# A transformer block on one core: attention spreads on two queues, halved score sums for the last chunk, and x loaded ahead of the weights

## The chip, the cores and the metric

The kernel runs on one core of a Trainium2 chip. The metric is the device time of one execution in microseconds (us). The names of the engines in the profile are PE (TensorE, matmuls), DVE (VectorE), ACT (ScalarE), POOL (GpSimd) and SP (SyncE, which here only issues DMA). DMAs are issued from the queues of SP, ACT and POOL.

## The reference

The block has 2048 positions of 512 features in bf16: a layer norm, a sliding dilated attention with 32 heads of 16 features, a residual, a second layer norm, a gated ReLU feed-forward layer with 1376 hidden features, and a residual.

```python
W, dil = 8, 2
idx = pos[:, None] - (jnp.arange(W) * dil)[None, :]      # 8 keys: s, s-2, ..., s-14
logits = einsum("bhsd,bhswd->bhsw", q, k[idx]) * Dh**-0.5  # masked where idx < 0
o = einsum("bhsw,bhswd->bhsd", softmax(logits), v[idx])
h = x + o @ wo
n = layernorm(h)
out = h + (relu(n @ W_gate) * (n @ W_up)) @ W_down
```

## The kernel before, in words

The positions are cut into four chunks of 512 (`tk` = 0 to 3). Features lie on partitions, positions along the free dimension. A chunk goes through these steps; the line numbers are those of the profile:

- layer norm 1: statistics on DVE (L466, L469), ln and exp on ACT (L479, L483), normalised rows on DVE (L501, chunks 0 and 2) or ACT (L498, chunks 1 and 3). The rows are transposed on PE (L530) and copied by ACT (L546) or, once, by DVE (L544). Chunk 3's four row blocks are instead transposed by DMAs on SP's queue (L519).
- q, k, v: matmuls (L571), copied out of PSUM by ACT (L579).
- q*k products on DVE. Chunks 1 to 3 use tiles of 128x4096 (L619), two feature groups by four window places by 512; chunk 0 uses halves of those (L634). A half `hf` of the window (four of the eight keys) takes two such tiles. They are summed over a head's features by matmuls with a 0/1 matrix `sel` (L625), 16 for each half; the exponential is on ACT (L683). In chunk 0 a small mask follows on DVE (L686).
- spreads: the exponentials (32 heads on 32 partitions per window place) are copied to 128 partitions by DMAs, `big<-ex` (L743), four for each half, 128 KB each. The table `BCD` names the queue of each: S is SP, A is ACT, P is POOL.
- a*v products on DVE (L775; halves in chunk 0, L790), summed over the window by a tree of adds (L778). In chunks 0 to 2 the first add, 128x2048, is a DMA with accumulation on POOL's queue (L818). The last step writes a tile of `quad` (L782 in chunk 0, L812 in the others).
- output projection on PE (L854), residual (L863, L865), layer norm 2, gate and up matmuls (L927, L894), their copies and product (L931, L934, L955), down matmuls (L977) and the second residual.

`setup()` issues the loads ahead of all that. SP and ACT each load a block of x, then a quarter of the q and k weights `wqk_sb`, twice. Three one-row copies on POOL (L333, L336, L338) read a piece of what has been loaded and write into a tile that is loaded next; so chunk 1's x, the v weights and the x of chunks 2 and 3 are not issued before the earlier loads have landed. `NFILL` matmuls on a dummy tile stand between the first transposes on PE.

The order of the work on each engine is written down: every step gets a number from the table `RANK`, and a list planner with durations for each kind of step puts the steps of each engine in order by it. Its durations are constants in the code. Every engine works strictly in its order, so a step that waits holds up all that stands behind it on its engine or queue.

Of the kernel before, what the change touches and what calls it, by code (L numbers as in the profile page):

```python
# [8 lines left out]
P = 128  # L9
# [193 lines left out]
def kernel(  # L203
# [22 lines left out]
    BCD = {(0,0):"SSSS",(0,1):"SSSS",(1,0):"SSSS",(1,1):"SSSS",(2,0):"SSSS",(2,1):"SSSS",(3,0):"SSSS",(3,1):"SSSS"}  # L226
    PRE = ()
    PRD = ()
    ODA = (0, 1)
# [82 lines left out]
    def setup():  # L312

        w3_r = A_wqkv.rearrange("(dt p) f -> p dt f", p=P)
        for i in range(2):
            for n, q in enumerate((nc.sync, nc.scalar)):
                j = 2 * i + n
                q.dma_start(x_sm[:, j:j + 1, :], x_rows[:, j:j + 1, :])
                q.dma_start(wqk_sb[:, j:j + 1, :], w3_r[:, j:j + 1, 0:2 * D])  # L319
# [13 lines left out]
        nc.gpsimd.tensor_copy(out=x_sm[0:1, BPC:2 * BPC, 0:1], in_=x_sm[0:1, 3, 0:BPC])  # L333
        for j in range(BPC, 2 * BPC):
            nc.sync.dma_start(x_sm[:, j:j + 1, :], x_rows[:, j:j + 1, :])
        nc.gpsimd.tensor_copy(out=wv_sb[0:1, 0, 0:1], in_=wqk_sb[0:1, 3, 0:1])  # L336
        nc.sync.dma_start(wv_sb[:], w3_r[:, :, 2 * D:3 * D])
        nc.gpsimd.tensor_copy(out=x_sm[0:1, 2 * BPC, 0:1], in_=x_sm[0:1, 2 * BPC - 1, 0:1])  # L338
# [34 lines left out]
    TDD, TDL = 1.25, 1.5  # L373
    NWARM, NFILL = 56, (13, 10, 0)
    NHALF = 6
    XT = (3.55, 3.4, 6.1, 5.85, 9.0, 9.3, 9.6, 10.0, 15.2, 16.75)
    WT = (7.7, 7.7, 5.6, 12.05, 18.0, 24.95, 21.45, 28.8)
# [4 lines left out]
    BDI = {"S": 0.63, "A": 0.65, "P": 0.95}  # L382
# [16 lines left out]
    MM, TP = 0.2165, 0.057  # L399
    SW = 0.21  # L400
    PEL = 0.22
    A5, A10, AX, AS = 0.485, 0.91, 0.75, 0.21
# [151 lines left out]
    for tk in range(NCK):  # L554
# [50 lines left out]
        for hf in range(2):  # L605
            sc, ex = Buf(at_s), Buf(ex_s)
            scd, prd = [], []
            for t in range(0, NT, 2):
# [13 lines left out]
                def f_sc(t=t, sc=sc, pb=pb):  # L622
                    for u in range(2):
                        for g in range(4):
                            nc.tensor.matmul(sc.t[g * HB:(g + 1) * HB, :], lhsT=sel[:],  # L625
                                             rhs=pb.t[:, 4 * u + g, :], start=(t + u == 0),
                                             stop=(t + u == NT - 1), tile_position=(0, g * HB))

                if tk in PRS:
                    def f_p1(u, t=t, hf=hf, pb=pb, qT=qT, s0=s0):  # L630
                        kb = kT[:, t + u, PADL + s0 - 4 * hf * DIL: PADL + s0 - 4 * hf * DIL + CS]
                        k4 = bass.AP(tensor=kb.tensor, offset=kb.offset,
                                     ap=[list(kb.ap[0]), [-DIL, 4]] + [list(y) for y in kb.ap[1:]])
                        V.tensor_tensor(out=pb.t[:, 4 * u:4 * u + 4, :],  # L634
                                        in0=qT.t[:, t + u, :].unsqueeze(1).to_broadcast([P, 4, CS]), in1=k4, op=ALU.mult)

                    for u in range(2):
                        a = add(("pr%d%s" % (hf, "ac"[u]), tk), "DVE", D20, lambda u=u, f=f_p1: f(u),
                                [d[t + u] for d in (qd, kd, kp)], apr, take=[pb], use=[qT], lat=DL)
                        prd.append((a, pb, f_sc if u else lambda: None))  # L640
                else:
                    a = add(("pr%d" % hf, tk), "DVE", D40, f_pr, [d[k] for k in (t, t + 1) for d in (qd, kd, kp)],
                            apr, take=[pb], use=[qT], lat=DL)
                    prd.append((a, pb, f_sc))
# [29 lines left out]
            elif tk in MERGE:  # L674
                scd = [add(("sc%d" % hf, tk), "PE", 4 * MM + SW, lambda p=prd: [f() for _, _, f in p],
                           [a for a, _, _ in prd], apr, take=[sc], use=[b for _, b, _ in prd], lat=PEL)]
            else:
                for a, pb, f in prd:
                    scd.append(add(("sc%d" % hf, tk), "PE", 2 * MM + SW, f, [a] + scd[-1:], apr,
                                   take=[sc], use=[pb], lat=PEL))  # L680
# [52 lines left out]
        for w0 in range(0, W, BCN):  # L733
            hf = w0 // 4
            if (tk, hf) in BCD:
                for eng, q in (("SP", nc.sync), ("ACT", nc.scalar), ("POOL", nc.gpsimd)):
# [4 lines left out]
                    def f_bd(ws=ws, q=q, w0=w0, ab=ab, ex=exs[hf]):  # L741
                        for w in ws:
# [3 lines left out]
                                   take=[ab], use=[exs[hf]], lat=0.77,  # L746
# [102 lines left out]
        for j in range(BPC):  # L849
# [20 lines left out]
            if tk in RPE:  # L870
                a = add(("rs%d" % j, tk), "ACT", 0.57, f_rs, [a], base + 50, take=[sm], use=[od], lat=AL)
            else:
                a = add(("rs%d" % j, tk), "DVE", 0.63, f_rs, [a], base + 50, take=[sm], use=[od], lat=DL)
# [190 lines left out]
```

## Time and profile before

| | |
|---|---|
| runs | 197.2, 198.14, 198.29 us; median 198.14 |
| profiled execution, first to last instruction | 199.0 us; the page gives no other time of it |
| busy: PE, DVE, ACT, POOL | 189.6 (95%), 147.9 (74%), 116.7 (59%), 17.7 us (9%) |
| q0 (POOL's DMA queue), q1 (SP's) | 7.34 and 16.23 MB; 20.2% and 29.7% of 16 engines' span |

The times in a row of the timeline are the start from the span's start and the duration in us; xN is the number of instructions merged into the row. In brackets stands how long the engine was idle before it and what ended that. In a group by line the columns are busy time, mean ns of one, and idle time before. `SPq` and `POOLq` rows are DMA issues.

### The profile page before, as it was taken

What the parts mean: (1) busy time and instruction counts of PE and PEld (TensorE: products, weight loads), DVE (VectorE), ACT (ScalarE), POOL (GpSimd) and SP (SyncE); (2) the same over time, 40 slices, a digit from 0 to 9 for tenths busy, and PEclk for the clock granted to TensorE, in tenths of its full rate; (3) what the DMA queues carried; (4) which work ended last, traced back from release to release, by engine and by line L of the source; (5) the groups of instructions that cost most, each with busy time, mean ns of one, the idle gap of its engine ahead of it and who ended that gap; (6) DMA issues with size and microseconds to landing.
All of it is one profiled execution on the core that took longest, in us unless ns stands there. A gap on an engine that the chain in (4) does not pass through costs nothing.

```text
span 199.0 us, 3083 instructions
## 1 busy us (share of the span) xinstructions
PE 189.6 (95%) x1120; PEld 98.5 (50%) x1139; DVE 147.9 (74%) x239; ACT 116.7 (59%) x241; POOL 17.7 (9%) x35
## 2 busy tenths in 40 slices
PE   8899998599999999999999999999999999999992
PEld 8895455245445534554444445544454544455451
DVE  6889999969969999999998769999954311214322
ACT  3579999326779676775536659606458725146300
POOL 3000002520000003300024010010010010000000
PEclk9999999879999999999999999999999999999999
DMA  6889386999600535967379973360030454000303
GB/s 207 231 274 381 96 183 126 190 187 350 217 0 0 137 78 105 190 127 160 80 146 174 188 174 65 65 120 3 0 53 8 103 178 110 0 0 0 109 6 126
DMA packets 25070, 24.61 MB, mean 124 GB/s; under 512 B 11136, under 2 KB 21344, under 8 KB 25056
## 3 DMA queue, kind: packets, MB, share of 16 engines
q1 hardware_dynamic: 22032, 16.23, 29.7%
q0 software_dynamic: 2304, 7.34, 20.2%
q10 hardware_dynamic: 720, 0.85, 1.2%
q8 instruction: 9, 0.15, 0.3%
q14 instruction: 5, 0.04, 0.1%
HBM read 8.42 MB, written 2.10 MB: 53 GB/s over the span
## 4 chain that ended last, share of the span: by engine, by line
PE 90%; DMA 5%; ACT 1%; issue 1%; DVE 1%; ACTq 0%
PE bank L927 34%; PE bank L571 20%; PE bank L977 19%; PE bank L854 7%; PE bank L625 4%; PE bank L894 3%; DMA quad<-row 3%; DMA x_sm<-in_A_x_dram 2%; PE bank L530 1%; ACT quad L579 1%; PE bank L857 0%; PE bank L700 0%; DVE st L466 0%; ACT lnd L706 0%; ACTq L319 0%
## 5 line engine op out<-in xcount | busy, mean ns | idle before, releaser
L927 PE MATMUL bank<-quad,wgu_sb 128*128 128x512 bf16 x311 | 72.0, 379 | 0.4
L927 PEld LDWEIGHTS <-wgu_sb 128*128 128x128 bf16 x320 | 31.0, 98 | 36.5 <-issue 0.8
L977 PE MATMUL bank<-wd_sb,gT 128*128 128x512 bf16 (+2 forms) x185 | 40.4, 367 | 0.2
L571 PE MATMUL bank<-quad,wqk_sb 128*128 128x512 bf16 (+1 forms) x149 | 31.2, 358 | 3.5 <-DMA quad<-row 3.1
L931 ACT CAST up_sb<-bank 128x512 bf16<-128x512 f32 x40 | 22.8, 589 | 19.5 <-PE bank L927 15.9
L934 ACT ACTIVATE gr<-bank 128x512 bf16<-128x512 f32 x40 | 23.3, 601 | 17.6 <-PE bank L927 10.9
L619 DVE TENSOR_TENSOR big<-quad,kT 128x4096 bf16<-128x4096 bf16 x12 | 27.2, 2284 | 2.4 <-ACT quad L579 2.2
L977 PEld LDWEIGHTS <-gT 128*128 128x128 bf16 (+1 forms) x187 | 18.1, 98 | 19.7 <-issue 0.4
L775 DVE TENSOR_TENSOR big<-big,vT 128x4096 bf16<-128x4096 bf16 x12 | 27.1, 2284 | 0.4 <-issue 0.2
L571 PEld LDWEIGHTS <-wqk_sb 128*128 128x128 bf16 x152 | 17.0, 115 | 15.1 <-issue 6.0
L955 DVE TENSOR_TENSOR gT<-gr,up_sb 128x1024 bf16<-128x1024 bf16 x20 | 13.7, 686 | 12.4 <-ACT up_sb L931 7.9
L990 DVE TENSOR_TENSOR row<-x_sm,bank 128x512 bf16<-128x512 bf16 (+1 forms) x9 | 5.5, 625 | 17.0 <-PE bank L977 17.0
L818 POOL DMA_DIRECT2D big<-big x12 | 10.5, 872 | 85.4 <-DVE big L775 59.8
L778 DVE TENSOR_TENSOR big<-big 128x1024 bf16<-128x1024 bf16 (+2 forms) x24 | 16.7, 728 | 0.8 <-DMA big<-big 0.8
L571 PE MATMUL bank<-quad,wv_sb 128*128 128x512 bf16 x61 | 15.7, 380 | 0.3 <-issue 0.2
L854 PE MATMUL bank<-wo_sb,quad 128*128 128x512 bf16 x62 | 14.9, 379 | 0.1
L579 ACT CAST vT<-bank 128x512 bf16<-128x512 f32 x16 | 9.0, 603 | 7.4 <-PE bank L571 7.4
L455 ACT ACTIVATE row<-x_sm,mv 128x512 bf16<-128x512 bf16 x12 | 8.5, 713 | 5.4 <-DVE mv L447 5.3
L466 DVE BATCH_NORM_STATS2 st<-x_sm 128x6 f32<-128x512 bf16 x16 | 10.3, 675 | 0.8 <-DMA x_sm<-in_A_x_dram 0.8
L546 ACT COPY quad<-bank 128x1024 bf16<-128x1024 bf16 (+1 forms) x10 | 8.5, 890 | 4.0 <-PE bank L530 4.0
L501 DVE TENSOR_SCALAR row<-x_sm,mv,rs 128x512 bf16<-128x512 bf16 x24 | 8.9, 406 | 2.5 <-ACT rs L483 2.5
L579 ACT CAST quad<-bank 128x512 bf16<-128x512 f32 x16 | 9.3, 593 | 2.3 <-PE bank L571 2.1
(77 smaller groups left out, 167.0 us busy)
## 6 DMA issues: line engine op xcount, KB each, us to landing
big<-big POOLq DMA_DIRECT2D x12, 512.0 KB, 5.4
big<-ex SPq DMA_DIRECT2D x32, 128.0 KB, 3.1
wgu_sb<-in_B_W_gate_dram SPq DMA_DIRECT2D x2, 688.0 KB, 9.2
wgu_sb<-in_B_W_up_dram SPq DMA_DIRECT2D x2, 688.0 KB, 6.0
wd_sb<-in_B_W_down_dram SPq DMA_DIRECT2D x2, 640.0 KB, 8.2
x_sm<-in_A_x_dram SPq DMA_DIRECT2D x2, 512.0 KB, 6.5
x_sm<-up_sb POOLq DMA_DIRECT2D x4, 256.0 KB, 3.4
out_dram<-x_sm SPq DMA_DIRECT2D x4, 256.0 KB, 3.1
```

The costliest lines, as they stand in the source:

```text
L571: nc.tensor.matmul(mm.t[:, lo:hi], lhsT=wv_sb[:, dt, t:D:NT] if c == 2 else wqk_sb[:, dt, c * D + t:(c + 1) * D:NT], rhs=xnT.t[:, dt, lo:h ...
L579: nc.scalar.copy(out=o, in_=mm.t[:])
L619: V.tensor_tensor(out=pb.t[:].rearrange("p (t w) s -> p t w s", t=2), in0=q4, in1=k4, op=ALU.mult)
L775: V.tensor_tensor(out=mt.t[:], in0=ab.t[:], in1=v8, op=ALU.mult)
L778: V.tensor_tensor(out=mt.t[:, 0:n, :], in0=mt.t[:, 0:n, :], in1=mt.t[:, n:2 * n, :], op=ALU.add)
L818: nc.gpsimd.dma_start(mt.t[:, 0:4, :], mt.t[:, 4:8, :], accum_op=ALU.add)
L854: nc.tensor.matmul(od.t[:], lhsT=OT.t[:, t, j * P:(j + 1) * P], rhs=wo_sb[:, t, :], start=(t == 0), stop=(t == NT - 1 and tk not in RPE))
L927: nc.tensor.matmul(mm.t[:fs, lo:hi], lhsT=wgu_sb[:, dt, g, ft * P: ft * P + fs], rhs=hnT.t[:, dt, lo:hi], start=(dt == 0), stop=(dt == NT ...
L931: nc.scalar.copy(out=ub.t[:fs, i, :], in_=um.t[:fs, :])
L934: nc.scalar.activation(out=gr.t[:fs, i, :], in_=gm.t[:fs, :], func=ACT.Relu)
L955: V.tensor_tensor(out=gt.t[:fs, 0:n, :], in0=gr.t[:fs, 0:n, :], in1=ub.t[:fs, 0:n, :], op=ALU.mult)
L977: nc.tensor.matmul(od.t[:, c0:c1], lhsT=gts[ft].t[:fs, ft % 2, j * P:(j + 1) * P], rhs=wd_sb[:fs, ft, c0:c1], start=(ft == 0), stop=(ft == ...
```

## The change

Four things change, and the order with them.

- `BCD`: in chunks 0 and 1 two of the four spreads of each half are issued by POOL.
- `PRH`: in chunk 3 each of the four q*k tiles gets a further step that adds its second feature group onto its first: half 1's two tiles on DVE, half 0's two by an accumulating DMA on POOL's queue. The matmuls with `sel` then run over half as many slices.
- `setup()`: all four x blocks of chunk 0 are issued ahead of the four weight quarters, and the three POOL copies are gone.
- `NFILL`, planner constants and the table `RANK`.

```diff
 RANK = [
-    20, 22, 23, 25, 28, 30, 31, 21, 24, 26, 27, 32, 35, 38, 40, 34, 39, 41, 43, 46,
+    20, 22, 23, 28, 30, 35, 36, 21, 24, 26, 27, 29, 33, 38, 37, 25, 31, 34, 39, 43,
...
-    BCD = {(0,0):"SSSS",(0,1):"SSSS",(1,0):"SSSS",(1,1):"SSSS",(2,0):"SSSS",(2,1):"SSSS",(3,0):"SSSS",(3,1):"SSSS"}
+    BCD = {(0, 0): 'SSPP', (0, 1): 'SSPP', (1, 0): 'SSPP', (1, 1): 'SSPP', (2, 0): 'SSSS', (2, 1): 'SSSS', (3, 0): 'SSSS', (3, 1): 'SSSS'}
+    PRH = {(3, 1, 0): 'V', (3, 1, 2): 'V', (3, 0, 0): 'D', (3, 0, 2): 'D'}
...
-        for i in range(2):
+        for i in (0, 2):
             for n, q in enumerate((nc.sync, nc.scalar)):
-                j = 2 * i + n
-                q.dma_start(x_sm[:, j:j + 1, :], x_rows[:, j:j + 1, :])
-                q.dma_start(wqk_sb[:, j:j + 1, :], w3_r[:, j:j + 1, 0:2 * D])
+                q.dma_start(x_sm[:, i + n:i + n + 1, :], x_rows[:, i + n:i + n + 1, :])
+        for i in (0, 2):
+            for n, q in enumerate((nc.sync, nc.scalar)):
+                q.dma_start(wqk_sb[:, i + n:i + n + 1, :], w3_r[:, i + n:i + n + 1, 0:2 * D])
...
-        nc.gpsimd.tensor_copy(out=x_sm[0:1, BPC:2 * BPC, 0:1], in_=x_sm[0:1, 3, 0:BPC])
         for j in range(BPC, 2 * BPC):
             nc.sync.dma_start(x_sm[:, j:j + 1, :], x_rows[:, j:j + 1, :])
-        nc.gpsimd.tensor_copy(out=wv_sb[0:1, 0, 0:1], in_=wqk_sb[0:1, 3, 0:1])
         nc.sync.dma_start(wv_sb[:], w3_r[:, :, 2 * D:3 * D])
-        nc.gpsimd.tensor_copy(out=x_sm[0:1, 2 * BPC, 0:1], in_=x_sm[0:1, 2 * BPC - 1, 0:1])
...
-    NWARM, NFILL = 56, (13, 10, 0)
+    NWARM, NFILL = 56, (8, 6, 0)
...
+                hs = PRH.get((tk, hf, t))
-                def f_sc(t=t, sc=sc, pb=pb):
-                    for u in range(2):
+                def f_sc(t=t, sc=sc, pb=pb, hs=hs):
+                    for u in range(1 if hs else 2):
...
+                    if hs == "D":
+                            nc.gpsimd.dma_start(pb.t[:, 0:4, :], pb.t[:, 4:8, :], accum_op=ALU.add)
+                    elif hs:
+                            V.tensor_tensor(out=pb.t[:, 0:4, :], in0=pb.t[:, 0:4, :], in1=pb.t[:, 4:8, :], op=ALU.add)
```

What this does to the order is shown at three places. First SP's queue around chunk 0's spreads, in the changed kernel and then before (`big_92` is the tile of the spread exponentials, `ex_100` and `ex_101` the two halves of the window, `quad_82` or `quad_83` chunk 3's normalised x):

```order
L311 DMA wgu_sb<-in_B_W_gate_dram 128x2x1376 x2
L754 DMA big_92<-ex_100 128x1x512 x2
L754 DMA big_92<-ex_101 128x1x512 x2
L518 DMA_TRANSPOSE quad_83<-row_108 128x4x128
L518 DMA_TRANSPOSE quad_83<-row_109 128x4x128
L518 DMA_TRANSPOSE quad_83<-row_105 128x4x128
L518 DMA_TRANSPOSE quad_83<-row_106 128x4x128
```

These are the changed kernel's; before, the same place reads:

```order
L310 DMA wgu_sb<-in_B_W_gate_dram 128x2x1376 x2
L743 DMA big_92<-ex_100 128x1x512 x4
L743 DMA big_92<-ex_101 128x1x512 x4
L519 DMA_TRANSPOSE quad_82<-row_108 128x4x128
L519 DMA_TRANSPOSE quad_82<-row_109 128x4x128
L519 DMA_TRANSPOSE quad_82<-row_105 128x4x128
L519 DMA_TRANSPOSE quad_82<-row_106 128x4x128
```

Four of eight spreads are gone from ahead of the transposes. They stand on POOL's queue, between the last of the setup and the accumulates of chunk 0 (`big_88` to `big_91` are its a*v products); first before, then changed:

```order
L330 MEMSET vT 128x4x16
L333 COPY x_sm<-x_sm 1x4
L336 COPY wv_sb<-wqk_sb 1x1
L338 COPY x_sm<-x_sm 1x1
L818 DMA big_89<-big_89 128x2048
L818 DMA big_88<-big_88 128x2048
L818 DMA big_91<-big_91 128x2048
L818 DMA big_90<-big_90 128x2048
```

In the changed kernel:

```order
L332 MEMSET vT 128x4x16
L754 DMA big_92<-ex_100 128x1x512 x2
L754 DMA big_92<-ex_101 128x1x512 x2
L829 DMA big_90<-big_90 128x2048
L829 DMA big_88<-big_88 128x2048
L829 DMA big_89<-big_89 128x2048
L829 DMA big_91<-big_91 128x2048
```

The copies have gone, the spreads of both halves have come ahead of the accumulates. The third place is DVE behind the mask of chunk 0's second half (`ex_101`), up to the two half products that the first accumulate needs; first before:

```order
L686 TENSOR_TENSOR ex_101<-ex_101,mask 128x16
L469 BN_AGGR mv_120<-st_115 128x2
L469 BN_AGGR mv_120<-st_117 128x2
L469 BN_AGGR mv_120<-st_116 128x2
L466 BN_STATS st_114<-x_sm 128x6
L466 BN_STATS st_115<-x_sm 128x6
L487 SCALAR_TENSOR_TENSOR nb_127<-mv_120,rs_132 128x4
L466 BN_STATS st_117<-x_sm 128x6
L466 BN_STATS st_116<-x_sm 128x6
L790 TENSOR_TENSOR big_89<-big_92,vT 128x2048
```

In the changed kernel:

```order
L697 TENSOR_TENSOR ex_101<-ex_101,mask 128x16
L465 BN_STATS st_115<-x_sm 128x6
L468 BN_AGGR mv_121<-st_115 128x2
L486 SCALAR_TENSOR_TENSOR nb_127<-mv_120,rs_132 128x4
L465 BN_STATS st_117<-x_sm 128x6
L801 TENSOR_TENSOR big_88<-big_92,vT 128x2048
L468 BN_AGGR mv_121<-st_117 128x2
L465 BN_STATS st_116<-x_sm 128x6
L465 BN_STATS st_114<-x_sm 128x6
L468 BN_AGGR mv_121<-st_116 128x2
L468 BN_AGGR mv_121<-st_114 128x2
L801 TENSOR_TENSOR big_90<-big_92,vT 128x2048 x2
```

The aggregations of chunk 3's statistics (`mv_120`) have moved ahead of the mask, and the first half product stands two statistics earlier, between those of chunk 2 (`mv_121`).

More of the change, by code (lines that the diff above doesn't have):

```diff
@@ L372 @@
     PRS, MUH = (0,), (0,)
-    TDD, TDL = 1.25, 1.5
-    NWARM, NFILL = 56, (13, 10, 0)
+    TDD, TDL = 1.3, 1.5
+    NWARM, NFILL = 56, (8, 6, 0)
     NHALF = 6
-    XT = (3.55, 3.4, 6.1, 5.85, 9.0, 9.3, 9.6, 10.0, 15.2, 16.75)
-    WT = (7.7, 7.7, 5.6, 12.05, 18.0, 24.95, 21.45, 28.8)
+    XT = (3.47, 3.64, 4.35, 4.5, 7.9, 8.2, 8.5, 8.8, 13.2, 14.7)
+    WT = (7.2, 7.2, 5.6, 12.0, 16.0, 24.95, 19.7, 28.8)
     DMAT = (('h',2,0),('h',2,2),('h',3,0),('h',3,2),('h',1,0),('x',3,0),('x',3,2))
     EARLY = (1, 2, 3)
-    BDI = {"S": 0.63, "A": 0.65, "P": 0.95}
+    BDI = {"S": 0.66, "A": 0.67, "P": 0.95}
     RPE, OPE = (0,), ()
@@ L396 @@
     LNA = ((0, 1, 0, 1), (0, 0, 0, 0))
-    MM, TP = 0.2165, 0.057
-    SW = 0.21
+    MM, TP = 0.216, 0.056
+    SW = 0.115
     PEL = 0.22
-    A5, A10, AX, AS = 0.485, 0.91, 0.75, 0.21
+    A5, A10, AX, AS = 0.48, 0.905, 0.72, 0.21
     AL = 0.13
@@ L626, in f_sc @@
                                              rhs=pb.t[:, 4 * u + g, :], start=(t + u == 0),
-                                             stop=(t + u == NT - 1), tile_position=(0, g * HB))
+                                             stop=(t == NT - 2 and bool(u or hs)), tile_position=(0, g * HB))
                 if tk in PRS:
@@ L643, with f_ph @@
                             apr, take=[pb], use=[qT], lat=DL)
+                    if hs == "D":
+                        def f_ph(pb=pb):
+                            nc.gpsimd.dma_start(pb.t[:, 0:4, :], pb.t[:, 4:8, :], accum_op=ALU.add)
+                        a = add(("ph%d" % hf, tk), "POOL", 1.0, f_ph, [a], apr, use=[pb], lat=1.1, dq=(0.75, 2.74))
+                    elif hs:
+                        def f_ph(pb=pb):
+                            V.tensor_tensor(out=pb.t[:, 0:4, :], in0=pb.t[:, 0:4, :], in1=pb.t[:, 4:8, :], op=ALU.add)
+                        a = add(("ph%d" % hf, tk), "DVE", D20, f_ph, [a], apr, use=[pb], lat=DL)
                     prd.append((a, pb, f_sc))
@@ L674 @@
             elif tk in MERGE:
-                scd = [add(("sc%d" % hf, tk), "PE", 4 * MM + SW, lambda p=prd: [f() for _, _, f in p],
+                scd = [add(("sc%d" % hf, tk), "PE", (4 - sum((tk, hf, t) in PRH for t in (0, 2))) * MM + SW, lambda p=prd: [f() for _, _, f in p],
                            [a for a, _, _ in prd], apr, take=[sc], use=[b for _, b, _ in prd], lat=PEL)]
@@ L745 @@
                     abd.append(add(("bd%d%s" % (hf, eng[0]), tk), eng, len(ws) * BDI[eng[0]], f_bd, [exd[hf]], apr + 1,
-                                   take=[ab], use=[exs[hf]], lat=0.77,
+                                   take=[ab], use=[exs[hf]], lat=0.97 if tk else 1.2,
                                    dq=(1.38 - BDI[eng[0]] * len(ws), 0.5 + BDI[eng[0]] * (len(ws) - 1))))
@@ L870 @@
             if tk in RPE:
-                a = add(("rs%d" % j, tk), "ACT", 0.57, f_rs, [a], base + 50, take=[sm], use=[od], lat=AL)
+                a = add(("rs%d" % j, tk), "ACT", 0.575, f_rs, [a], base + 50, take=[sm], use=[od], lat=AL)
             else:
-                a = add(("rs%d" % j, tk), "DVE", 0.63, f_rs, [a], base + 50, take=[sm], use=[od], lat=DL)
+                a = add(("rs%d" % j, tk), "DVE", 0.73, f_rs, [a], base + 50, take=[sm], use=[od], lat=DL)
             hd.append((a, od))
```

72 rows, old and new, of the table RANK are left out of this document.

## The prediction

> **What bounds the kernel now.** First the profile's page and its chain that ended last, then the same chain in order of time, then busy time by stage.
>
> ```profile
> span 199.0 us, 3083 instructions
> PE 90%; DMA 5%; ACT 1%; issue 1%; DVE 1%; ACTq 0%
> ```
> ```profile
> 8.32 0.60 PE bank L571 x4
> ...
> 31.79 5.28 DMA quad<-row
> 37.20 5.09 PE bank L571 x15
> 42.34 10.74 PE bank L571 x49
> ...
> 53.73 0.98 PE bank L625 x16
> ```
> ```profile
> core 0: us, PE busy (x) PEld busy (x) DVE busy (x) ACT busy (x) POOL busy (x), PEclk, DMA share, GB/s
> 8.32:34.14 25.82, 25.54 (x191) 16.32 (x194) 24.76 (x47) 22.99 (x45) 1.18 (x2) 1.00 0.75 212
> 34.14:37.20 3.06, 0.00 (x0) 0.03 (x1) 3.06 (x4) 2.53 (x4) 0.86 (x1) 1.00 1.05 201
> 37.20:42.34 5.14, 5.09 (x15) 2.12 (x17) 5.14 (x7) 0.00 (x0) 2.86 (x3) 0.67 1.03 193
> 60.00:100.00 40.00, 39.79 (x248) 18.86 (x251) 39.60 (x52) 27.51 (x60) 3.44 (x4) 1.00 0.53 111
> 100.00:140.00 40.00, 39.79 (x199) 19.07 (x201) 35.63 (x50) 22.30 (x46) 5.16 (x6) 1.00 0.59 114
> ```
>
> From 8.3 us to the end TensorE (PE) sets the time, with one hole: 34.14 to 37.20, 3.06 us without a matmul. Behind it the granted clock is 0.67, so 15 matmuls took 5.09 us; the 49 behind them took 10.74, or 0.219 each. At that rate 15 take 3.3 us, so the slow clock cost 1.8 us. VectorE (DVE) is as full as PE up to 42 us and from 60 to 100, so whatever PE gains DVE has to follow. What ended the hole is told by the waits and the timeline:
>
> ```profile
> PE bank L571 <- DMA quad<-row: 3.1, 1, 3.1
> ```
> ```profile
> 21.63 6.04 SPq L743 DMA_DIRECT2D big<-ex  x8
> 23.97 0.15 DVE L686 TENSOR_TENSOR ex<-ex,mask 128x16 bf16<-128x16 bf16 x1
> 24.26 1.25 DVE L466 BATCH_NORM_STATS2 st<-x_sm 128x6 f32<-128x512 bf16 x2
> 25.61 1.52 ACT L498 ACTIVATE row<-x_sm,nb,rs 128x512 bf16<-128x512 bf16 x2 [0.38 <-DVE nb L487]
> 27.50 1.53 ACT L498 ACTIVATE row<-x_sm,nb,rs 128x512 bf16<-128x512 bf16 x2
> 27.77 5.24 SPq L519 DMA_TRANSPOSE quad<-row  x4
> 31.64 1.01 POOL L818 DMA_DIRECT2D big<-big  x1 [21.61 <-PE bank L571]
> ```
> ```profile
> L519 SPq DMA_TRANSPOSE quad<-row x4: 1199/1216/1319, 27.8 to 31.8; - x4
> DMA to landing us min/median/max: 2.4/2.6/5.3
> ```
>
> Chunk 3's normalised rows go through four DMA transposes on SyncE (SP). The first row is there at about 26.4 us, but SP is busy with chunk 0's eight spreads until 27.67. The transposes then take 1.31 us of issue each; the last is issued at 31.79, beside the first 512 KB accumulate of GpSimd (31.64), and lands 5.3 us later instead of 2.4. That is the hole.
>
> **The start.**
>
> ```profile
> 5.98 0.69 DVE L466 BATCH_NORM_STATS2 st<-x_sm 128x6 f32<-128x512 bf16 x1 [0.48 <-DMA x_sm<-in_A_x_dram]
> 6.59 0.40 DVE L501 TENSOR_SCALAR row<-x_sm,mv,rs 128x512 bf16<-128x512 bf16 x1
> 7.67 0.18 POOL L336 COPY wv_sb<-wqk_sb 1x1 bf16<-1x1 bf16 x1 [1.47 <-DMA wqk_sb<-in_A_wqkv_dram]
> 7.79 0.39 DVE L544 COPY quad<-bank 128x512 bf16<-128x512 bf16 x1
> ```
>
> DVE waits 0.48 us for the third x block before it can normalise the second row (6.59); PE's first real matmul (8.32) waits for that row's transpose and its copy, which ends at 8.18. wqk's last quarter is there at 7.67, when the GpSimd copy that waits for it starts. With x ahead of the weights the third block is there when DVE asks, but in the new order its statistics stand ahead of both rows, and the fourth block's ahead of the copy. Counting: statistics 3 at 5.1, rows at 5.8 and 6.2, aggregation and statistics 4 until 7.35, the copy until 7.8. So the first matmul comes at 7.9, 0.4 us earlier (bounds: 0, if wqk's quarters come later behind x; 1.0, if DVE's pieces overlap better). The nine fewer fill matmuls stand before it and save nothing by themselves. That chunk 1's x and wv are no longer held back takes no place from wqk on the path: they are behind it on SP's queue. **0.4 us.**
>
> **The spreads of chunk 0 and the hole.** SP has four issues instead of eight, 4 x 0.755 (6.04 over 8) = 3.0 us less. The second half's two cannot start before its mask, at about 24.7 instead of 23.97: three more aggregations of 0.1 stand ahead of it, and the first scores, which start this stretch, have four more matmuls ahead (0.86, less the 0.4 gained); so SP is free at 24.8 + 1.5 = 26.3. The first row is there at 26.4 (its chain, mask, statistics, `nb`, ACT, is within 0.1 us of before). Four transposes at 1.31: the last issued at 30.3, done issuing at 31.6, landing at 30.3 + 2.6 = 32.9. GpSimd's first accumulate needs both halves of a product; DVE's row count from the mask at 24.8 is four statistics (0.63 each, half of 1.25), three half products (1.13 each, half of a full one below), aggregations and `nb` (0.7): 6.6, so 31.4. Its data meets only the last transpose's tail. PE reaches the place at 34.14 - 0.4 = 33.7, with the same matmuls before it. Four rows of chunk 2 are also needed there, ready at 31.4 + 4 x 0.4 = 33.0. So the hole shrinks from 3.06 to about 0.2 us (bounds 0 and, if the last transpose still lands 5.3 us after its issue, 35.6 - 33.7 = 1.9). **2.9 us**, and with no hole of 3 us no slow clock: **1.8 us**.
>
> What GpSimd's own spreads cost, no row shows. Nearest are its accumulates against SP's spreads:
>
> ```profile
> big<-big POOLq DMA_DIRECT2D x12, 512.0 KB, 5.4
> big<-ex SPq DMA_DIRECT2D x32, 128.0 KB, 3.1
> ```
> ```profile
> L818 POOL DMA_DIRECT2D big<-big x12 | 10.5, 872 | 85.4 <-DVE big L775 59.8 <-PE bank L571 21.6 <-DVE big L790 3.9
> ```
>
> Issue 0.87 us; landing between 3.1 (same bytes) and 5.4 (same engine, four times the bytes). I take 3.5, nearer to the row with the same bytes. Chunk 0's first half: second issue 22.6, landed 26.1, wanted by DVE at 27. Second half: 25.7 + 3.5 = 29.2, wanted at about 30.
>
> **Does DVE follow?** Its durations:
>
> ```profile
> 72.87 4.49 DVE L775 TENSOR_TENSOR big<-big,vT 128x4096 bf16<-128x4096 bf16 x2 [0.18 <-DVE big L619]
> 111.47 1.29 DVE L778 TENSOR_TENSOR big<-big 128x1024 bf16<-128x1024 bf16 x2
> 88.77 1.09 DVE L812 TENSOR_TENSOR quad<-big 128x512 bf16<-128x512 bf16 x3
> 45.07 4.49 DVE L619 TENSOR_TENSOR big<-quad,kT 128x4096 bf16<-128x4096 bf16 x2 [2.20 <-ACT quad L579]
> 91.00 3.62 PE L854 MATMUL bank<-wo_sb,quad 128*128 128x512 bf16 x16
> ```
>
> So 2.25 us a full product, 0.64 an add of 1024, 0.36 a row of 512. Adding the new order's rows from 33.0: chunk 1's second q*k product is done at 45.6, chunk 0's last output tile at 47.9, the fourth q*k product at 52.4. PE asks for them at 33.7 + 64 matmuls x 0.219 = 47.7, at 48.7, and after four output blocks (4 x 1.08) at 53.0. The 2.20 us that DVE waited at 45.07 for ACT, itself held by the hole, are used. Onward to chunk 1's outputs stand five q*k and four a*v products (20.3), seven rows of 1024 (4.5), ten of 512 (3.6), four normalised rows (1.6) and small ones (0.4): 30.4, so 82.8. PE asks at 91.00 less 5.1 gained and less 8 matmuls (1.75) that now stand behind: 84.1. By the same count chunks 2 and 3 come about 1 us ahead of PE. Margins of 0.6 to 2 us are little; but before, from 60 to 140, PE lost 0.4 us in all. I take **-0.5 us** (bounds 0 and -2).
>
> **Chunk 3's scores.** Its four q*k tiles are added half to half, so each score step has 8 matmuls instead of 16. By the row of 53.73, 16 take 0.98; two steps save 2 x 0.49 = **1.0 us** of PE, which is busy there, so on the path. The price: two adds of 128x2048 on DVE (twice an add of 1024, 1.2 us each) and two accumulates of 512 KB on GpSimd's queue. DVE's 2.4 us lie between 100 and 140, where it had 4.4 us idle, and are in the counts above. The accumulates (5.4 to land) begin when the second tile is done, near 85, and the score step stands at 95. Cover gone, that step would wait at most 2 us.
>
> **Sum**, against the profiled span: 0.4 + 2.9 + 1.8 + 1.0 - 0.5 = 5.6 us, span 193.4. The page gives no other time of that execution; the runs' median, 198.14, is 0.9 below its span, so I take 198.14 - 5.6 = 192.5. Own range: all good bounds 0.6 + 0.2 + 0.5 better, 191.2; bad bounds 0.4 + 1.7 + 1.5 worse, 196.1.
>
> **Rivals.**
>
> *The hole stays.* The transposes come earlier, but so may the first accumulate, and if GpSimd's spreads and SP's share the DMA engines the last transpose meets it again; the DMA share was 1.05 in the hole. Against: 1.6 us more room by the count. Then only 0.4 + 1.0 is won: 196.7.
>
> *Slower: GpSimd's spreads are late.* They are queued behind one another (0.87 each) on the engine that also issues the accumulates, and DVE, full until 100, has nothing to do until the last lands. The longest landing of a GpSimd transfer is in chunk 0's accumulates:
>
> ```profile
> DMA to landing us min/median/max: 4.7/5.2/7.0
> ```
>
> At 7.0, chunk 0's first half lands at 29.6, 2.6 us late, and PE gets chunk 2's rows that much later: the hole and its slow clock are back. In chunk 1 the four issues start at 57.6, the last at 60.3, landing at 67.3 where DVE wants 64.2: 3.1 late, less the 1.3 of margin, 1.8 us of PE, and if PE's waits lie together the slow clock once more, 1.8. Sum: -1.4 + 1.8 + 1.8 = +2.2, **200.3**. It decides from a landing of about 6.5 us; at 5.4 the forecast loses 1 to 2 us. For it: a GpSimd copy beside DVE's work took 1.27 us, another 0.22:
>
> ```profile
> 41.20 1.27 POOL L836 COPY wgu_sb<-big 1x4 bf16<-1x4 bf16 x1 [2.05 <-DVE big L778]
> 42.40 0.22 POOL L837 COPY wd_sb<-big 1x11 bf16<-1x11 bf16 x1
> ```
>
> Against: all twelve accumulate issues took 0.87 on the mean beside a full DVE. The Trainium skill, "SBUF — State Buffer", section "Who interferes with whom", has a rule that speaks against the change: a DMA issued from GpSimd has its descriptors written by GpSimd, and DVE instructions in a two-port mode (`tensor_scalar`, copies) lock it out until they end, while `tensor_tensor` does not. By that rule chunk 1's spreads, which stand beside four `tensor_scalar` rows, would wait for each (0.4 us) and land at most 1.6 us later, 0.3 more than the margin; the accumulates stand mostly beside `tensor_tensor`, so the trace doesn't contradict it.
>
> *The change does little.* If the first row for the transposes, not SP, ended last at 27.7, the transposes would not move: but it is there at 26.4 in the rows above. The result would be that of "the hole stays".
>
> **How the numbers follow.** No change means within 0.5% (1.0 us), the spread of the runs. Forecast 0.56, the hole stays 0.20, the spreads late 0.19, gains and losses even 0.05. Faster by over 0.5% is below 197.15: all of the forecast and three quarters of "the hole stays", 0.71. Same: the rest of that and the even case, 0.10. Slower 0.19. The range takes in forecast and hole from 190.8 to 198.5 and leaves out the slower rival.
>
> **What would show it.** Right: no PE gap over 1 us at chunk 3's first matmul, clock 1.00 from 34 to 45, four score steps' worth of 16 fewer matmuls, first real matmul near 7.9, and DVE without a wait for `big<-ex`. Wrong: DVE waiting for `big<-ex` at a product, the transposes again landing after 35 us, or a second stretch of granted clock under 1.

## The result, and the profile after

The changed kernel takes **202.72 us** (median of 4 runs, 201.69 to 203.72), against 198.13 (197.2 to 198.29) for the kernel before, run beside it: a ratio of 1.0236, 95% interval 1.0201 to 1.027. It is 4.6 us slower; the prediction was 192.5.

The profiled execution is the shortest of the four: 201.69 us, 1.0 below the median, at a full mean clock. First busy time by stage, in the stages of the prediction and in two around the loss:

```profile
span 199.6 us, 3039 instructions
```
```profile
core 0: us, PE busy (x) PEld busy (x) DVE busy (x) ACT busy (x) POOL busy (x), PEclk, DMA share, GB/s
34.14:37.20 3.06, 2.98 (x23) 1.71 (x20) 3.06 (x4) 3.06 (x6) 1.24 (x2) 1.00 0.78 150
37.20:42.34 5.14, 5.14 (x25) 2.71 (x24) 5.14 (x6) 4.11 (x9) 2.06 (x3) 1.00 1.01 190
80.00:95.00 15.00, 15.00 (x75) 7.07 (x74) 12.56 (x30) 9.87 (x24) 1.71 (x2) 1.00 1.00 188
95.00:105.00 10.00, 6.02 (x38) 2.37 (x36) 8.64 (x8) 3.36 (x5) 2.10 (x3) 1.00 0.33 56
100.00:140.00 40.00, 39.51 (x205) 18.19 (x206) 36.42 (x48) 22.53 (x46) 6.99 (x8) 1.00 0.61 125
```

The hole at 34.14 to 37.20 is gone and the clock behind it is 1.00, as forecast. A new hole stands at 95 to 105: PE is busy for 6.02 of 10 us. The stage ahead of it, 80 to 95, has a DMA share of 1.00. The timeline of PE, and below it DVE's, tell what ended the waits:

```profile
8.29 0.93 PE L570 MATMUL bank<-quad,wqk_sb 128*128 128x256 bf16 x6 [0.47 <-DMA wqk_sb<-in_A_wqkv_dram]
...
99.03 0.40 PE L529 MATMUL bank<-identity,row 128*128 128x128 bf16 x4 [2.92 <-DVE row L500]
100.00 0.40 PE L529 MATMUL bank<-identity,row 128*128 128x128 bf16 x4 [0.57 <-DVE row L500]
...
104.15 2.10 PE L938 MATMUL bank<-quad,wgu_sb 128*128 128x512 bf16 x9 [0.49 <-DMA quad<-row]
```
```profile
68.20 4.49 DVE L786 TENSOR_TENSOR big<-big,vT 128x4096 bf16<-128x4096 bf16 x2 [2.06 <-DMA big<-ex]
...
92.25 0.35 DVE L915 TENSOR_TENSOR row<-gr,bank 128x192 bf16<-128x192 bf16 x1
96.36 2.29 DVE L786 TENSOR_TENSOR big<-big,vT 128x4096 bf16<-128x4096 bf16 x1 [3.76 <-issue]
98.57 1.38 DVE L500 TENSOR_SCALAR row<-x_sm,mv,rs 128x512 bf16<-128x512 bf16 x4
```

PE lost 2.92 + 0.57 + 0.49 = 3.98 us. For 3.49 of these it waited for chunk 2's normalised rows (L500), which stand on DVE behind chunk 2's first a*v product (L786); DVE stood idle for 3.76 us before that product. The word "issue" names no releaser. The answer on the line of the spreads (L754), from 78 to 92 us, names the spreads, and the rows of POOL show what runs beside them. In an answer on a line the columns are the engine's minimum, median and maximum in ns, and the first and last start:

```profile
L754 SPq DMA_DIRECT2D big<-ex x8: 543/602/2184, 81.8 to 89.1; - x8
who waited for it (us, times):
  DVE big L786: 3.8, 1
DMA to landing us min/median/max: 2.8/6.2/7.1
```
```profile
80.53 0.86 POOL L647 DMA_DIRECT2D big<-big  x1 [1.95 <-DVE big L618]
88.36 0.85 POOL L647 DMA_DIRECT2D big<-big  x1 [6.97 <-DVE big L618]
```

Chunk 2's eight spreads, all on SP as before, are issued between the two new accumulates of chunk 3. One issue takes 2184 ns instead of some 550, and half of the spreads land 6.2 us or more after their issue. An issue at 89.1 that lands 7.1 later ends at 96.2: DVE starts at 96.36. Before, chunk 2's eight spreads (88.3 to 93.7) landed after 2.7 in the median and 3.5 at most, with no accumulate issued between 83.0 and 100.9.

### The profile page after: what moved, and what is told of

Its sections match the earlier page's. It is cut to its first block, busy times and chain, and to the rows that moved or that the text cites. A ratio compares the mean times of both kernels' runs of the same rounds, so it can differ in the third digit from the quotient of the medians.

```text
span 199.6 us, 3039 instructions
## 1 busy us (share of the span) xinstructions
PE 189.8 (95%) x1114; PEld 97.9 (49%) x1114; DVE 150.0 (75%) x241; ACT 115.4 (58%) x241; POOL 25.4 (13%) x42
## 4 chain that ended last, share of the span: by engine, by line
PE 52%; DVE 9%; DMA 6%; issue 5%; SPq 2%; ACT 2%; DVEq 0%; POOL 0%; ACTq 0%
PE bank L938 29%; PE bank L988 14%; DVE big L618 5%; DMA big<-ex 4%; PE bank L865 3%; DVE big L786 3%; PE bank L905 2%; SPq L754 2%; DMA quad<-row 2%; PE bank L570 1%; PE bank L626 1%; DVE row L500 1%; DVE gT L966 1%; ACT kT L578 1%; ACT quad L578 0%
## 5 line engine op out<-in xcount | busy, mean ns | idle before, releaser
L988 PE MATMUL bank<-wd_sb,gT 128*128 128x512 bf16 (+3 forms) x187 | 39.2, 366 | 0.0
L786 DVE TENSOR_TENSOR big<-big,vT 128x4096 bf16<-128x4096 bf16 x12 | 27.1, 2285 | 5.8 <-issue 3.8
L570 PE MATMUL bank<-quad,wqk_sb 128*128 128x512 bf16 (+1 forms) x152 | 30.2, 346 | 0.6 <-DMA wqk_sb<-in_A_wqkv_dram 0.6
L578 ACT CAST kT<-bank 128x512 bf16<-128x512 f32 x16 | 9.2, 607 | 3.4 <-PE bank L570 2.3
L801 DVE TENSOR_TENSOR big<-big,vT 128x2048 bf16<-128x2048 bf16 x8 | 9.4, 1213 | 1.1 <-ACT row L497 1.1
L500 DVE TENSOR_SCALAR row<-x_sm,mv,rs 128x512 bf16<-128x512 bf16 x24 | 8.5, 408 | 2.2 <-ACT rs L482 2.2
```

Source lines behind the costliest of these rows:

```text
L570: nc.tensor.matmul(mm.t[:, lo:hi], lhsT=wv_sb[:, dt, t:D:NT] if c == 2 else wqk_sb[:, dt, c * D + t:(c + 1) * D:NT], rhs=xnT.t[:, dt, lo:h ...
L578: nc.scalar.copy(out=o, in_=mm.t[:])
L786: V.tensor_tensor(out=mt.t[:], in0=ab.t[:], in1=v8, op=ALU.mult)
L988: nc.tensor.matmul(od.t[:, c0:c1], lhsT=gts[ft].t[:fs, ft % 2, j * P:(j + 1) * P], rhs=wd_sb[:fs, ft, c0:c1], start=(ft == 0), stop=(ft == ...
```

## The experiments

Theory: the two 512 KB accumulates of chunk 3 on GpSimd's queue delay chunk 2's spreads. Rivals: GpSimd's spreads in chunks 0 and 1, the load order, the fuller DVE. A second question is where the forecast gains went. All ratios are to the kernel before, run beside it.

### What costs the time

**e2: neither accumulate.** The half-0 tiles of chunk 3 are summed whole, as before.

```diff
-                            nc.gpsimd.dma_start(pb.t[:, 0:4, :], pb.t[:, 4:8, :], accum_op=ALU.add)
+                            pass
```

> The changed kernel without the two GpSimd accumulates on chunk 3's half-0 tiles; the score step of that half sums all 16 slices again, order unchanged. Theory A (the second accumulate, issued at 88.4 us, delays chunk 2's spreads, DVE waits 3.8 us and PE 3.5 us, and in most runs the clock halves after it): the gap at 96 to 99 us goes, 0.5 us of matmuls come back, time 202.7 - 3.5 - about 1.2 (slow clock) + 0.5 = 198.5. Theory B (GpSimd's spreads are the loss): 203.2.

Measured: 196.82 us (195.8 to 197.6), ratio 0.9968 (0.9937 to 0.9999). The loss is gone, 5.9 us. It is 1.7 below Theory A's 198.5. The same stage, the same answers on the spreads' line, and DVE's and PE's timelines at the place of the loss:

```profile
80.00:95.00 15.00, 15.00 (x75) 7.07 (x74) 14.97 (x32) 10.10 (x24) 0.00 (x0) 1.00 0.58 124
```
```profile
L755 SPq DMA_DIRECT2D big<-ex x8: 543/556/608, 82.1 to 86.6; - x8
DMA to landing us min/median/max: 2.5/2.6/2.8
```
```profile
92.73 2.29 DVE L787 TENSOR_TENSOR big<-big,vT 128x4096 bf16<-128x4096 bf16 x1
...
96.17 0.61 PE L529 MATMUL bank<-identity,row 128*128 128x128 bf16 x8
```

The DMA share from 80 to 95 us is 0.58 instead of 1.00. The last spread is issued at 86.6 and lands by 89.4; DVE wants it at 92.73. So there are 3.3 us of slack.

**e3: all spreads on SP**, the accumulates kept.

```diff
-                            q.dma_start(ab.t[:, w0 + w, :], ...)
+                            nc.sync.dma_start(ab.t[:, w0 + w, :], ...)
```

> The changed kernel with all spreads of chunks 0 and 1 issued by SP again, at the same places in the order. Theory A (the loss is the accumulate at 88 us): 202.7, within 1 us. Theory B (GpSimd's spreads land late, 5.1 us instead of 3.1, and cost DVE 2.1 us at 66 us): 200.5 or less, and no wait for the spreads before chunk 1's first a*v product. Against both: chunk 3's transposes start later again and the hole at 34 us is back, then over 204.

Measured: 201.4 us (200.0 to 201.75), ratio 1.0192 (1.0116 to 1.0267). The loss stays without a single spread on GpSimd, in PE's timeline with nearly the same row (the median is 1.3 us below the changed kernel's, but the two intervals overlap):

```profile
97.39 0.40 PE L529 MATMUL bank<-identity,row 128*128 128x128 bf16 x4 [2.81 <-DVE row L500]
```

**e5: the earlier accumulate only (80.6 us); e13: the later only (88.3 us).** The tile without one is summed whole. The diff of e5 (e13 has `t == 2` and `if not t`):

```diff
+                he = None if hs == "D" and t == 0 else hs
-                def f_sc(t=t, sc=sc, pb=pb, hs=hs):
+                def f_sc(t=t, sc=sc, pb=pb, hs=he):
...
+                            if t:
+                                nc.gpsimd.dma_start(pb.t[:, 0:4, :], pb.t[:, 4:8, :], accum_op=ALU.add)
```

> The changed kernel with only the earlier of the two accumulates (issued at 80.5 us); the one issued at 88.4 is dropped and its tile is summed over all slices. Theory A (the second one's transfer delays chunk 2's spreads): DVE's 3.8 us wait goes, 196.6. Theory B (both accumulates cost, since the first one already fills the DMA engines from 81 us on and pushes everything behind it): about 199.5.

> The changed kernel with only the later of its two accumulates, the one at 88.4 us; the other tile is summed whole by 16 matmuls. With neither the time was 196.8, with the earlier alone 197.2, with both 202.7. Theory A (both are needed): the earlier one holds SP's issue of the spreads back (last issue 89.1 instead of 86.6), the later one makes the landing of what is still under way long; alone it meets only the last one or two spreads, they land before 93 us: about 197. Theory B (the later alone does it): landing of chunk 2's last spreads 6 to 7 us, DVE waits 1 us or more behind 92.6: 199 to 202.

Measured: e5 197.17 us (196.42 to 197.62), ratio 0.9976 (0.9949 to 1.0003); e13 197.06 (196.18 to 197.35), 0.9962 (0.9935 to 0.9989). The spreads of chunk 2 in e5, then in e13:

```profile
L756 SPq DMA_DIRECT2D big<-ex x8: 543/598/2225, 82.0 to 89.3; - x8
DMA to landing us min/median/max: 2.6/4.3/6.9
```
```profile
L756 SPq DMA_DIRECT2D big<-ex x8: 542/560/617, 81.8 to 86.3; - x8
DMA to landing us min/median/max: 2.6/2.7/2.8
```

Either alone costs nothing that is measured. The earlier one makes one of SP's issues take 2225 ns and moves the last from 86.6 to 89.3. The later one alone, at 88.3, finds all spreads issued and landing in 2.8 us or less. The 6.9 us in e5 are those of the first spread, beside the earlier accumulate, not of the last. The answers for the last three alone (window 88.4 to 89.6), in the changed kernel and then in e5, tell them apart:

```profile
L754 SPq DMA_DIRECT2D big<-ex x3: 594/594/610, 87.8 to 89.1; - x3
DMA to landing us min/median/max: 2.8/6.7/7.1
```
```profile
L756 SPq DMA_DIRECT2D big<-ex x3: 594/594/602, 88.0 to 89.3; - x3
DMA to landing us min/median/max: 2.6/2.6/2.6
```

Only with both do the late last spreads meet the later accumulate: issued 89.1 - 86.6 = 2.5 us later and landing up to 7.1 - 2.8 = 4.3 later, 6.8 in all, less 3.3 of slack: 3.5 us, and DVE was idle for 3.76.

**e6 and e14: accumulates of 128 and 256 KB instead of 512.** The kernels leave out a part of chunk 3's score sums.

```diff
-  ... pb.t[:, 0:4, :], pb.t[:, 4:8, :], accum_op=ALU.add
+  ... pb.t[:, 0:1, :], pb.t[:, 4:5, :], accum_op=ALU.add     (e6)
+  ... pb.t[:, 0:2, :], pb.t[:, 4:6, :], accum_op=ALU.add     (e14)
```

> The changed kernel with both accumulates over one slice of 512 instead of four (128 KB instead of 512; the scores then leave out three quarters of the second feature groups). Same order, same issues, same waits. Theory A (the bytes on the DMA engines are the cost): chunk 2's spreads land within 4 us, 196.5. Theory B (the accumulate's issue, its place on GpSimd's queue or the score step's wait for it): 202, as the changed kernel.

> The changed kernel with accumulates of 256 KB instead of 512 (it leaves out half of the second feature groups in two score sums of chunk 3). Quarters gave 197.3, full size 202.7. Theory A (the loss is a wait that begins when the delay passes 3.4 us of slack before DVE wants the spreads): the last spread lands near 92 us, no wait: 197.0 to 197.8. Theory B (the loss grows with the bytes): about 199.

Measured: e6 197.27 us (195.96 to 197.78), ratio 0.9988 (0.9957 to 1.002); e14 197.81 (196.61 to 198.84), 1.0 (0.9968 to 1.0033). Landing of chunk 2's spreads in e6, then in e14:

```profile
DMA to landing us min/median/max: 2.5/2.7/4.0
```
```profile
DMA to landing us min/median/max: 2.6/3.3/5.5
```

By bytes of each accumulate: 0, 128, 256, 512 KB give 196.8, 197.3, 197.8, 202.7. The longest landings grow with the bytes, but in e6 and e14 they are those of the first spreads, beside the earlier accumulate. The last spreads are issued at 86.9 and 86.8, ahead of the later accumulate (88.01 and 87.42), and land after 2.6 us, long before DVE wants them (92.16 and 91.57). So e14's last spread lands at 89.4, not near 92 as Theory A had it. Theory A's time came, but the last spreads don't drift towards the end of the slack as the bytes grow: the time jumps at 512 KB, where the earlier accumulate holds SP back so long that the last two spreads meet the later one. In e14's profile, its shortest execution, DVE doesn't wait there; its other executions are 0.8 to 2.2 us longer, and where they lose that was not seen.

**e8: the same adds on DVE.**

```diff
-                            nc.gpsimd.dma_start(pb.t[:, 0:4, :], pb.t[:, 4:8, :], accum_op=ALU.add)
+                            V.tensor_tensor(out=pb.t[:, 0:4, :], in0=pb.t[:, 0:4, :], in1=pb.t[:, 4:8, :], op=ALU.add)
```

> The changed kernel with the two accumulates turned into adds on DVE at the same places (1.2 us each). Theory A (bytes on the DMA engines are the cost, but DVE has no slack before 100 us: without the accumulates chunk 1's output tiles are done as PE asks for them): the spreads' delay goes, DVE is 1.2 to 2.4 us later, 196.8 - 0.5 + about 1.8 = 198.1. Theory B (DVE has slack there): 196.3.

Measured: 198.93 us (197.96 to 200.0), ratio 1.0075 (1.0043 to 1.0106), 2.1 above e2. Two adds of 1.2 us come out as 2.1 us of the whole: DVE has no room in this stretch, and from 80 to 95 us it is busy for 15.00 of 15.00. PE then waits for it, as in this row of its timeline:

```profile
86.70 3.63 PE L865 MATMUL bank<-wo_sb,quad 128*128 128x512 bf16 x16 [0.70 <-DVE quad L823]
```

### Where the forecast gains went

**e1: the kernel before**, unchanged, with a trace of another execution.

> The kernel before, unchanged, to see how its executions differ from one another. Theory A (the profiled execution of before was not a typical one: the timed runs are about 2 us above their own span, so the usual span is near 196.2, not 199.0, and the hole at 34 us with its slow clock is mostly absent): spans 195.3 to 196.5, mean granted clock 1.00, PE idle at chunk 3's first matmul under 1 us, time 198.1. Theory B (the hole is always there and the time lies below the span): spans near 199, clock 0.991, time 198.1.

Measured: 198.2 us (197.53 to 199.93), ratio 1.003 (0.9991 to 1.007). Its profiled execution took 197.91 us with a span of 196.1: the time is 1.8 above the span, as in most runs since (median 1.8, from 1.7 to 3.0). The execution on which the prediction was built, with its span of 199.0, was therefore one of about 200.8 us. Such executions exist but are few: of 114 of the kernel before, taken with these experiments, nine have a mean clock of 0.991 or less, as the profiled one (0.991), and take 199.9 to 202.3 us. In e1 the rows of the start and of the hole read

```profile
6.99 0.69 DVE L466 BATCH_NORM_STATS2 st<-x_sm 128x6 f32<-128x512 bf16 x1 [1.50 <-DMA x_sm<-in_A_x_dram]
```
```profile
9.34 0.60 PE L571 MATMUL bank<-quad,wqk_sb 128*128 128x256 bf16 x4 [0.33 <-ACT rs L479]
35.96 3.62 PE L571 MATMUL bank<-quad,wqk_sb 128*128 128x512 bf16 x16 [0.74 <-DMA quad<-row]
```

The hole is 0.74 us, not 3.06, and 16 matmuls behind it take 3.62 us: no slow clock. The third x block is late by 1.50 us, not 0.48.

**e11: the kernel of e2 with all spreads on SP**, by the edit of e3.

> The changed kernel without its two accumulates of chunk 3 (196.8 us), now with all spreads on SP. Theory A: SP's eight issues put chunk 3's transposes later, and a hole of 2 to 3 us stands in PE near 34 us, or DVE waits for the eight issues in chunk 1: 198 to 199. Theory B: SP can take them all and only the accumulates cost time: 196.8.

Measured: 196.96 us (195.87 to 197.57), ratio 0.9975 (0.9953 to 0.9998), as e2. In the new order GpSimd's spreads buy nothing. The transposes of chunk 3 and the first accumulate, by their rows:

```profile
L518 SPq DMA_TRANSPOSE quad<-row x4: 1200/1216/1336, 27.8 to 31.9; - x4
DMA to landing us min/median/max: 2.4/2.5/2.7
```
```profile
33.20 1.01 POOL L830 DMA_DIRECT2D big<-big  x1 [30.76 <-PE bank L570]
```

The transposes stand where they stood before (27.8 to 31.8), but land within 2.7 us: the accumulate comes at 33.20 instead of 31.64, so 1.3 us behind the last transpose's issue instead of just ahead of it. In the new order SP's relief is therefore not needed to take the hole away. That the order alone does it is not shown: e11 has the new loads too, and e4 below has no hole in the old order with SP relieved.

DVE's wait for chunk 1's spreads is there as well without a spread on GpSimd, 1.54 us instead of 2.06:

```profile
67.29 6.70 DVE L787 TENSOR_TENSOR big<-big,vT 128x4096 bf16<-128x4096 bf16 x3 [1.54 <-DMA big<-ex]
```

**e7: the kernel of e2 with before's order of loads; e12: before with the new one.** The edit is the part of the change in `setup()`.

> The changed kernel without the accumulates (as in an earlier run, 196.8) and with the loads and the three GpSimd copies of before. Theory A (the new load order gives nothing, since the first matmul waits for the weights that now come behind x): 196.8 within 0.5. Theory B (the prediction's: 0.4 us gained at the start): 197.2, first real matmul 0.4 later.

> The kernel before with the new order of loads alone. Theory A: it is worth what it was in the new order, 1.35 us: 196.7, with the first real matmul 0.5 to 1.5 us earlier. Theory B: the hole at 34 us takes the gain back, since chunk 3's rows and transposes are not earlier by as much: 197.5 to 198.1.

Measured: e7 198.17 us (197.03 to 199.69), ratio 1.0036 (1.0001 to 1.0071), 1.35 above e2; e12 197.59 (196.45 to 198.26), 1.0013 (0.9991 to 1.0036). The loads are worth 1.35 us in the new order and nothing measurable in the old. They are not won at the first real matmul, as Theory B had it: that comes at 8.00 in e7 and at 8.07 in e2. Two waits of PE in e7 stand behind it, for the v weights and for chunk 1's normalised row:

```profile
15.02 1.05 PE L572 MATMUL bank<-quad,wv_sb 128*128 128x512 bf16 x4 [0.30 <-DMA wv_sb<-in_A_wqkv_dram]
16.43 0.40 PE L531 MATMUL bank<-identity,row 128*128 128x128 bf16 x4 [0.36 <-ACT row L499]
```

e2 has neither, and the first score matmuls come at 21.18 in e7 and at 20.46 in e2: 0.72 of the 0.8 us by which the two spans differ. So what pays is probably that the v weights and chunk 1's x are no longer held back; no run separates that from x ahead of the weights. What takes the gain back in e12 was not found: its profile is of one of its two shortest executions.

**e4: before, with two of four spreads of chunks 0 and 1 on GpSimd; e9: that with the new loads; e10: e9 with GpSimd in chunks 2 and 3 too.** The edit of e4 and e9 (`tk < 4` in e10):

```diff
-                            q.dma_start(ab.t[:, w0 + w, :], ...)
+                            (nc.gpsimd if tk < 2 and w > 1 else q).dma_start(ab.t[:, w0 + w, :], ...)
```

> The kernel before with its own order, and only the spreads changed: two of four of each half in chunks 0 and 1 go to GpSimd's queue. Theory A (spreads are not the loss): 198.1 within 0.7, chunk 3's transposes start 1.3 us earlier. Theory B (GpSimd's spreads cost): over 200.

> The kernel before, in its own order, with two of the change's parts: x ahead of the weights without the three GpSimd copies, and two of the four spreads of each half of chunks 0 and 1 on GpSimd. The spreads alone gave 196.3 us (1.8 less than before). Theory A: the loads' order is worth about 1.35 us here too, as between the two runs without the accumulates that differ in it (196.8 and 198.2), and the parts add: 195.0, first real matmul near 8.0 us, no hole at 34 us. Theory B: the gain of the loads' order belongs to the new order of steps; here 196.3.

> The one with loads and GpSimd spreads in the order of before, and GpSimd spreads in chunks 2 and 3 too. Theory A: what hurt in the change was the 512 KB accumulates beside the spreads, not GpSimd as issuer; GpSimd's spreads land within 5 us in chunks 2 and 3 too: 194.5 to 195.5. Theory B: GpSimd's queue is behind its accumulates there; spreads land later than 6 us and DVE waits 1 to 2 us for them in chunk 2 or 3: over 196.

Measured: e4 196.31 us (195.12 to 197.59), ratio 0.9938 (0.99 to 0.9977); e9 197.04 (196.11 to 198.35), 0.9984 (0.9959 to 1.0009); e10 **195.77** (195.66 to 195.88), 0.9927 (0.9899 to 0.9955). In the old order GpSimd's spreads help by 0.6%, which neither theory of e4 had: PE has no hole at 34 us there. The parts don't add: e9 gains less than e4, and neither theory's time came. With all chunks' spreads shared the kernel is faster than both kernels of this case, and PE has no row with a wait between its first real matmul and 190 us. GpSimd's spreads in chunk 2 of e10:

```profile
L741 POOL DMA_DIRECT2D big<-ex x4: 541/562/599, 84.3 to 88.4; - x4
DMA to landing us min/median/max: 2.8/4.4/4.8
```

Why e9 stays behind both was not settled; in e9's profile PE waits 0.90 us at 129 us, in e10's it doesn't. The new order by itself brings nothing here: with the old loads and GpSimd's spreads in both, e7 (ratio 1.0036) is 1% slower than e4 (0.9938); with the new loads e2 (0.9968) and e9 (0.9984) are alike. `NFILL` and the planner's constants had no run of their own.

## Why the prediction was wrong

From 192.5 to 202.72 are 10.2 us. The two accumulates are 5.9 of them; without them (e2, 196.82) the kernel is still 4.3 above the forecast, and that is mainly the hole with its clock.

- **Chunk 3's scores (+1.0): the step that failed.** Its words were "Cover gone, that step would wait at most 2 us". The accumulates were costed only by the score step that reads their result, which indeed never waited. The accumulates themselves took 7.9 and 6.6 us to land instead of the 5.4 taken. What they do to others was not costed: SP's spreads of chunk 2 lie between them. The prediction had explained the old hole by just this, an accumulate beside a transposing DMA (5.3 us to land instead of 2.4), and didn't ask for the same at 80 to 95 us. The trace of before had a price for it: chunk 3's spreads there, behind the last accumulate of chunk 2, land after 5.5 us in the median and 7.1 at most, with one issue of 1738 ns. The prediction took the median of all 32, 3.1.

```profile
108.47 0.86 POOL L818 DMA_DIRECT2D big<-big  x1 [1.34 <-DVE big L775]
```
```profile
L743 SPq DMA_DIRECT2D big<-ex x8: 543/606/1738, 109.2 to 117.4; - x8
DMA to landing us min/median/max: 3.2/5.5/7.1
```

PE's waits make 4.0 us in the profiled execution; e2 and the median of the changed kernel are 5.9 apart. Of the rest, 1.0 is the distance of the profiled execution from the median. The clock fits it: three of the four executions have a mean granted clock of 0.98, the profiled one 1.00. That the clock falls behind the new hole, as it did behind the old one, is argued; no trace shows it. About a microsecond stays unexplained. The Trainium skill, "DMA: Bandwidth & Descriptors", section "Queues, rings and completion order", has each DMA engine take packets from its queues in turn; that agrees with landings that grow with the accumulates' bytes (2.8, 4.0, 5.5, 7.1 us at most for 0, 128, 256, 512 KB).

- **The hole and its clock (2.9 + 1.8).** The hole went, and with it the slow clock, but the size did not hold: a usual execution has 0.74 us there and a full clock (e1). Nor did the count of SP's queue: the last transpose was to be issued at 30.3, and was at 31.9, no earlier than before, because ACT starts the last of the four rows only at 30.97:

```profile
L518 SPq DMA_TRANSPOSE quad<-row x4: 1205/1216/1834, 27.3 to 31.9; - x4
DMA to landing us min/median/max: 2.4/2.4/3.7
```

What kept the two apart is the first accumulate, at 33.59 where 31.4 was counted. So the right outcome came in part by luck: "SP has four issues instead of eight" is not needed in this order (e11).

- **The base.** "0.9 below its span" set a median against the span of an untypical execution. Time lies 1.7 us or more above the span, which would have marked the profiled one as a long one; the page alone did not give that.
- **The start (0.4).** In the two profiles the first real matmul came at 8.32 and 8.29: the lower bound, "if wqk's quarters come later behind x", as PE's 0.47 us for wqk shows. Executions of before differ here (9.34 in e1). What the loads do bring, 1.35 us (e7), comes behind the first real matmul, and probably from the part that the prediction put at nothing: chunk 1's x and the v weights, which are no longer held back.
- **GpSimd's spreads.** Taken as 3.5 us, they landed after 3.6 to 4.3 in chunk 0 and 3.1 to 5.3 in chunk 1. "DVE without a wait for `big<-ex`" fell: DVE waited 2.06 us at 68.20. But 1.54 of such a wait are there with all spreads on SP (e11), so GpSimd's part is about 0.5 us. PE lost as much behind it, in a row that e3 and e11 don't have and every other profile of the new order has (0.42 to 0.65 us):

```profile
78.72 6.20 PE L938 MATMUL bank<-quad,wgu_sb 128*128 128x512 bf16 x28 [0.54 <-ACT gr L945]
```

That is the slower rival's mechanism at a seventh of its price (1.8 us, and 1.8 more for the clock). The rule of the Trainium skill, "SBUF — State Buffer", section "Who interferes with whom", that DVE's two-port instructions lock GpSimd's descriptor writes out, can't be read off here: the four issues of chunk 1 (60.7 to 62.4) took 546 to 579 ns, the first of them beside four `TENSOR_SCALAR` rows (60.37 to 61.75), and where GpSimd's spreads landed after up to 5.3 us, SP's own took up to 5.8 in the same stretch.

- **Does DVE follow (-0.5).** Nearly: up to the new hole PE's waits for DVE and ACT are 0.21, 0.15 and 0.54 us, 0.9 in all.
- **The rivals.** The slower one named the right end and the wrong place: the spreads that came late were SP's, in chunk 2, and e3 shows the loss without GpSimd's spreads. No rival had the accumulates.

## What to carry to other kernels

A DMA that is added to a queue is costed by what stands on the other queues at the same time, not only by who reads its result: list the transfers under way in its window and how much slack each has. A delay below the slack costs nothing and one above it costs at once, so two changes that are free alone can cost 5 us together, as here. Read the longest landing of such a transfer, not only the median: the trace of before had 7.1 us beside 3.1. Before a hole is priced from one trace, set that execution's time against the median, and ask whether the hole is there in another one.

## What the runs showed of the hardware that was not expected

- A 512 KB accumulating DMA on GpSimd's queue lengthens not only landings but SP's issue: one 128 KB spread took 2184, 2225 and 1990 ns to issue where an accumulate was under way (changed kernel, e5, e3) and at most 608 in e2. The kernel before had this too (1738 ns behind the accumulate at 108.47). An accumulate is not the only cause: one issue of chunk 2's spreads before took 1339 ns, when the last accumulate had landed (83.0 + 5.7 = 88.7).
- The wait that this causes is shown on DVE as "issue", without a releaser; only the answer on the line of the spreads named who waited for it.
- A GpSimd copy of 1x4 elements took 3.39 us at 41.66 in the changed kernel and 1.27 before. DVE waited 0.25 us behind it, at 45.24; no row of PE waits for it or for the weights loaded behind it.
